# Two heads of a pair in the other order, and global scores as one block-diagonal product

## The chip, the cores and the metric

The kernel runs on one core of a Trainium2 chip. Its engines are TensorE (the matrix unit, PE in the profile; its weight loads are shown as PEld), VectorE (DVE), ScalarE (ACT), GpSimd (POOL) and SyncE (SP, which issues the transfers here). TensorE multiplies a stationary operand of up to 128 rows by 128 columns with a moving operand and adds into PSUM, from where DVE and ACT read. The metric is the device time in microseconds of one execution.

## The reference

Four sequences (B = 4) with 8 heads of 64 each hold 512 local and 32 global tokens. Global queries attend to all 544 keys; local ones attend to the 32 global keys and to a window of 32 keys on either side. The result, 2304 tokens of 512 features, goes through two feed-forward stages:

```python
s_g = scale * np.matmul(q_g, k_all.transpose(0, 1, 3, 2))     # global scores
out_g = np.matmul(sm(s_g), v_all)
s_ll = np.where(mask, scale * np.matmul(q_l, k_l.transpose(0, 1, 3, 2)), -1e9)
a_l = sm(np.concatenate([s_lg, s_ll], axis=-1))               # s_lg: local queries on global keys
out_l = np.matmul(a_l, np.concatenate([v_g, v_l], axis=2))
...
h = np.maximum(x @ w_in, 0.0);  y = h * h @ w_out             # 512 -> 2048 -> 512
a, b = y @ w1, y @ w2                                         # 512 -> 1024
out = (a * b @ w3) @ w_out2                                   # -> 512
```

## The kernel before, in words

**Stages.** The kernel starts with attention of the first sequence and converts the first MLP's weights. Then a main list, the MLP's units for the blocks of one sequence (`h_unit`, first matrix, and `x_unit_a`, second matrix), is merged with a list of steps of attention for the next sequence (`cycle`, `merge`). So attention of sequences 1 to 3 runs beside the MLP of sequences 0 to 2, and all attention is over after some 330 us. Then follow the rest of the first MLP, the product of the last two matrices (`w_unit`), and the second MLP (`p_unit`, `x_add`).

**Pairs of heads.** The heads of a sequence are treated two at a time: pair j holds the heads 2j and 2j+1, called head 0 and head 1 in what follows. Queries and keys of a pair lie in one tile, head 0 in the rows 0 to 63, head 1 in the rows 64 to 127 (`ROWS`), with 64 features each. A product of one head's queries and keys thus uses 64 of TensorE's 128 rows, and two heads' products can run side by side. The first sequence (pairs 0 to 3) works on float32 as it was loaded (`kq_f`); one float32 product is two instructions in the trace. From pair 4 on, `emit_k` splits the raw tile (`kqraw`, two buffers) into a high and a low part (`kq_hl`, type float32r) on DVE, and a product is the sum of three passes, high by high, high by low, low by high (`PASSES`), of one instruction each. `emit_k` of pair n+1 is issued in the cycle of pair n, and then asks for the raw tile of the pair after.

**Steps of a pair.**
- `emit_g` (L213): scores of the 32 global queries of both heads against all keys, in two pieces of 288 and 256 keys. Before the change it reads the unsplit float32 tile for every pair. Four products, head by piece, are issued in turn so that the two heads work on different pieces; each takes 64 rows and 32 columns of the array, a quarter of its width. Softmax follows on DVE and ACT, into `pg`.
- `emit_s` (L200): scores of local queries, for 256 of them (a part), two groups of 128, into one PSUM tile for each head (`sc`); `soft` turns them into probabilities `p` (DVE, ACT, then a scaling on POOL at L195).
- `emit_t` (L261) transposes `p` of one head on TensorE (`tp`), and ACT copies it to `pt`; `emit_tg` does the same for `pg` (`tg`).
- `emit_pv` (L274): the products with the values, both heads into one PSUM tile `o`, head 0 in rows 0 to 63, head 1 in rows 64 to 127.
In a cycle the steps of pair n (global scores, local scores) and those of pair j = n-1 (transposes, value products) alternate; head 1's transposes of a part come after head 0's, just ahead of the value products of the second part.

**What sets the order.** The program order gives priorities, and a planner that simulates the engines' times places each instruction on its engine as soon as its operands and buffers are there in the simulation. So an instruction early in the program that must wait lets later ones pass. `in_turn` (L105) pins each product of a list behind the one before it, from the second product on; the first is free. On the chip each engine then takes its instructions in that order. The PSUM tiles `sc`, `sg`, `tg`, `tp` and `o` share one tag, `at`, with four buffers.

**POOL's work** in this stretch: the sums of converted weights (L395), the scaling (L195), squares (L434) and low parts (L103) for the MLP.

Of the kernel before, what the change touches and what calls it, by code (L numbers as in the profile page):

```python
# [9 lines left out]
F32 = mybir.dt.float32  # L10
F32R = mybir.dt.float32r
# [9 lines left out]
B, H, SL, SG, D = 4, 8, 512, 32, 64  # L21
S = SL + SG
# [29 lines left out]
HALF = 256  # L52
# [22 lines left out]
def attention_mlp(ctx: ExitStack, tc: tile.TileContext, kq0, kq, vw, wts, mask, ident, out):  # L75
    nc = tc.nc
# [9 lines left out]
    cv, rot, at = cv_cm.__enter__(), rot_cm.__enter__(), at_cm.__enter__()  # L86
# [4 lines left out]
    mask_sb = rot.tile([128, 4, 256], BF16, name="mask_sb")  # L91
    pg = rot.tile([128, 6, 128], F32, name="pg")


    sts = [rot.tile([128, 10], F32, name=f"st{k}") for k in range(ST_BUFS)]
    stgs = [rot.tile([64, 8], F32, name=f"stg{k}") for k in range(2)]
# [5 lines left out]
    def split_lo(eng, lo, raw, hi):  # L102
        eng.tensor_tensor(out=lo, in0=raw, in1=hi.bitcast(F32), op=ALU.subtract)  # L103

    def in_turn(products):  # L105

        for k, (o, w, x, start, stop) in enumerate(products):
            m = mm(o, w, x, start=start, stop=stop)  # L108
            if k:
                tc.keep_in_program_order(m)  # L110

    def chain(o, terms):
        for k, (w, x) in enumerate(terms):
            mm(o, w, x, start=(k == 0), stop=(k == len(terms) - 1))  # L114
# [4 lines left out]
    def xb(b):  # L119

        if b not in x_t:
            x_t[b] = sb.tile([128, 4, 2 * NB], F32, tag="xb", name="xb", bufs=2)
        return x_t[b]

    ROWS = [slice(64 * h, 64 * h + 64) for h in range(2)]
    kq_raw, kq_t, qg_t, v_t, p_t, pt_t = {}, {}, {}, {}, {}, {}

    def kq_tile(name, dtype=F32):
        return rot.tile([128, S + NK], dtype, tag="kq", name=name, bufs=KQ_BUFS)

    def load_pair(j, part):

        if part == 0:
            kq_raw[j] = kq_tile("kq_f32")
        t = kq_raw[j]
        c = slice(0, 608) if part == 0 else slice(608, HALF + NK + SG + HALF)
        nc.sync.dma_start(out=t[:, c], in_=kq0[j, :, c])  # L140
        q, k = t[:, :HALF] if part == 0 else t[:, HALF + NK :], t[:, HALF : HALF + NK]
        kq_t[j, part] = [(q, k)]
        qg_t[j] = q[:, :SG], k

    def load_kq(j):

        if H <= 2 * j < B * H:
            t = kq_raw[j] = pools["cv"].tile([128, S + NK], F32, tag="kqraw", name="kqraw", bufs=2)
            for h, r in enumerate(ROWS):
                src = kq[2 * j + h - H, r]  # L150
                nc.sync.dma_start(out=t[r, :HALF], in_=src[:, :HALF])
                nc.sync.dma_start(out=t[r, HALF:S], in_=src[:, HALF + NK :])
                nc.sync.dma_start(out=t[r, S:], in_=src[:, HALF : HALF + NK])
# [9 lines left out]
    def emit_k(j):  # L163

        raw = kq_raw.pop(j)
        hi, lo = (kq_tile("kq_hl", F32R) for _ in range(2))
        nc.vector.tensor_copy(hi, raw)
        split_lo(nc.vector, lo, raw, hi)
        for part, c in enumerate((slice(0, HALF), slice(HALF, S))):
            both = [(t[:, c], t[:, S:]) for t in (hi, lo)]  # L170
            kq_t[j, part] = [(both[a][0], both[e][1]) for a, e in PASSES]
        qg_t[j] = raw[:, HALF : HALF + SG], raw[:, S:]
        load_kq(j + 1)

    def soft(i, part, sc):
# [24 lines left out]
    def emit_s(j, part):  # L200

        terms = kq_t[j, part]
        sc = [ps.tile([128, 2, 256], F32, tag="at", name="sc", bufs=AT_BUFS) for _ in ROWS]
        at_q, at_k = (128 * n + SG * part for n in range(2)), KSTART[2 * part : 2 * part + 2]
        in_turn(
            (o[:, n, :], x[r, c : c + 128], y[r, w : w + 256], k == 0, k == len(terms) - 1)
            for n, (c, w) in enumerate(zip(at_q, at_k))
            for k, (x, y) in enumerate(terms) for o, r in zip(sc, ROWS)
        )
        for h, o in enumerate(sc):  # L210
            soft(2 * j + h, part, o)

    def emit_g(j):  # L213

        q, keys = qg_t.pop(j)
        sg = [ps.tile([128, 512], F32, tag="at", name="sg", bufs=AT_BUFS) for _ in range(2)]

        pf = pg.rearrange("p c k -> p (c k)")
        tail = pf[:, 288:736].rearrange("p (a c) -> p a c", a=2)[:, :, :128]
        pieces = (  # L220
            (sg[0][:, :288], lambda x: x[:, :288], pf[:, :288]),
            (
                sg[1][:, :256].rearrange("p (a c) -> p a c", a=2),
                lambda x: x[:, 256:576].rearrange("p (a c) -> p a c", a=2)[:, :, 32:160],
                tail,
            ),
        )
        products = []
        for turn in range(2):
            for h, r in enumerate(ROWS):  # L230
                s, of_keys, _ = pieces[(turn + h) % 2]
                products.append((s[SG * h : SG * (h + 1)], q[r], of_keys(keys[r]), True, True))
        in_turn(products)
        st = stgs[j % 2]
        for k in range(2):
            nc.vector.tensor_reduce(
                out=st[:, k : k + 1], in_=sg[k][:64, : 256 + 32 * (1 - k)], axis=AX.X, op=ALU.max
            )
        nc.vector.tensor_reduce(out=st[:, 2:3], in_=st[:, 0:2], axis=AX.X, op=ALU.max)
        nc.vector.tensor_scalar_mul(st[:, 2:3], st[:, 2:3], -SCALE)  # L240
        for k, (s, _, p) in enumerate(pieces):
            nc.scalar.activation(
                p[:64], s[:64], AF.Exp, bias=st[:, 2:3], scale=SCALE, accum_out=st[:, 3 + k : 4 + k]
            )
        nc.vector.tensor_reduce(out=st[:, 6:7], in_=st[:, 3:6], axis=AX.X, op=ALU.add)
        nc.vector.reciprocal(st[:, 6:7], st[:, 6:7])
        nc.vector.tensor_scalar_mul(pf[:64, :640], pf[:64, :640], st[:, 6:7])
# [26 lines left out]
    def emit_pv(j, part, alone=False):  # L274

        b, heads = 2 * j // H, (2 * j, 2 * j + 1)
        o = ps.tile([128, 2, 160], F32, tag="at", name="o", bufs=AT_BUFS)


        both, local, glob = slice(0, 160), slice(0, 128), slice(128, 160)  # L280
        if part == 0:
            m = local if alone else both
            groups = ((0, 0, m), (0, 1, m)), ((1, 6, local), (1, 7, local))
        else:
            more = (0, 1, 4) if alone else (4,)
            groups = (
                ((0, 2, both), *((0, c, glob) for c in more), (0, 3, both)),
                ((1, 5, local), (1, 4, local)),
            )
        in_turn(  # L290
            (o[r, n, m], v_t[i][:, VPOS[c], :], pt_t[i][:, c, m], k == 0, k == len(g) - 1)
            for g in groups for k, (n, c, m) in enumerate(g) for i, r in zip(heads, ROWS)
        )
        s = part * (HALF + SG)
        x = xb(b)[:, j % (H // 2)]
        nc.scalar.copy(x[:, s : s + HALF].rearrange("p (n q) -> p n q", n=2), o[:, :, :128])
        g = x[:, HALF : HALF + SG]
        if part == (1 if alone else 0):
            nc.vector.tensor_copy(g, o[:, 0, 128:])
        elif part == 1:  # L300
            nc.vector.tensor_tensor(out=g, in0=g, in1=o[:, 0, 128:], op=ALU.add)
        if part == 1 or alone:
            for i in heads:
                del pt_t[i], v_t[i]
# [17 lines left out]
    def cycle(j, ahead=True, behind=True):  # L322
# [31 lines left out]
        if ahead and not native and n + 1 < B * H // 2:  # L354
            steps.insert(3, lambda: emit_k(n + 1))
# [143 lines left out]


    load_pair(0, 0)
    nc.sync.dma_start(out=mask_sb, in_=mask)
    nc.sync.dma_start(out=ident_sb, in_=ident)
    load_pair(1, 0)
    load_w(0)
    load_v(0, 0)
    load_v(1, 0)
    load_w(1)
    load_pair(2, 0)
    load_pair(3, 0)  # L510
    load_v(2, 0)
# [3 lines left out]
    for t in stgs:  # L515
        nc.gpsimd.memset(t, 1e-9)
    nc.vector.memset(pg, 0.0)

    def xcols(i):
        s, n = block(i)  # L520
        s -= S * (i // 2)
        return x_t[i // 2][:, :, s : s + n]
# [18 lines left out]
    def end_a(i, d, o):  # L541
        (nc.scalar.copy if d < 2 or i < SHARED else nc.vector.tensor_copy)(staged(i, d), o)
        if d == 3:
            nc.sync.dma_start(out=of(part_d, i), in_=st_t[0])

    def split_a(i, d):
        if i < NBLK:
            split_x(i, d, xcols(i)[:, d])
        else:
            split_x(i, d, x_t[0][:, 0, d])  # L550
# [12 lines left out]
    for i in range(0, NBLK, 2):  # L563
        main = []
        for j in (i, i + 1):
            if j >= SHARED:
                main += rows(
                    j, 0, 8, lambda d, j=j: split_a(j + 1, d), lambda d, j=j: end_a(j, d, acc[d])
# [204 lines left out]
```

## Time and profile before

| | |
|---|---|
| median of three runs | 925.94 us (922.17 to 926.93) |
| the profiled execution | 921.11 us, span 919.0 us |
| TensorE, its weight loads | busy 891.2 us (97%), 789.2 us (86%) |
| DVE, ACT, POOL | 398.2 us (43%), 478.2 us (52%), 284.8 us (31%) |
| mean granted TensorE clock | 0.994 |

The span runs from the first to the last instruction of the profiled execution. In the timeline a row gives start and length in us, engine, line, operation, what is written and read, the part of the array (128*64: 128 rows and 64 columns), the moving operand, and how many instructions were merged into the row. The end of a TensorE row is modelled and lies a little behind the start of the next.

### The profile page before, as it was taken

Reading aid. Unit: us, or ns where it says so; the run is one execution under the profiler, and the core shown is the slowest. Engines: PE = TensorE matmul, PEld = TensorE weight load, DVE = VectorE, ACT = ScalarE, POOL = GpSimd, SP = SyncE. Lnnn points to the kernel's source line nnn. Section 1 sums busy time; section 2 is a strip of 40 time slices with the busy share of each in tenths; the row PEclk is TensorE's granted clock in tenths of the full one; section 3 lists DMA queues with packets and bytes.
Section 4 is the critical chain, followed back from the end, with each engine's and each line's share of the span. In section 5 each row is a group of like instructions: output and inputs, shape, how many; then the busy total and the mean of one; then the engine's idle time right before and its main releaser. Section 6 shows DMA issues by size and latency. Waiting matters only on the chain.

```text
span 919.0 us, 15988 instructions
## 1 busy us (share of the span) xinstructions
PE 891.2 (97%) x6128; PEld 789.2 (86%) x6128; DVE 398.2 (43%) x1019; ACT 478.2 (52%) x1235; POOL 284.8 (31%) x280
## 2 busy tenths in 40 slices
PE   6799999999999999999999999999999999999998
PEld 3577787888888899999988899999988888888886
DVE  6996554563164336676544456564010200201201
ACT  6887666756375657886655558764111211212111
POOL 4594541635163522322222222210111111111111
PEclk9899999999999999999999999999999999999999
DMA  7643313232124227335544445545000200100101
GB/s 253 217 133 92 97 49 123 74 98 95 50 52 132 79 73 237 130 133 180 191 144 166 162 136 182 180 158 169 1 24 1 87 1 0 44 1 1 44 1 43
DMA packets 52347, 92.58 MB, mean 101 GB/s; under 512 B 4400, under 2 KB 35248, under 8 KB 52272
## 3 DMA queue, kind: packets, MB, share of 16 engines
q1 hardware_dynamic: 52272, 91.57, 30.3%
q8 instruction: 48, 0.79, 0.3%
q14 instruction: 27, 0.22, 0.1%
HBM read 71.63 MB, written 19.92 MB: 100 GB/s over the span
## 4 chain that ended last, share of the span: by engine, by line
PE 68%; ACT 10%; DMA 10%; DVE 5%; POOL 3%; issue 2%; SPq 1%; ACTq 0%; POOLq 0%; DVEq 0%
PE ab L114 21%; PE acc L465 15%; PE h L114 12%; DMA wraw<-in_wts 9%; PE x L114 7%; PE o L108 4%; PE sc L108 3%; PE tp L267 3%; ACT wt L372 2%; PE sg L108 2%; POOL wt L395 2%; ACT wt L375 2%; DVE wt L385 2%; ACT r L431 1%; ACT hl L432 1%
## 5 line engine op out<-in xcount | busy, mean ns | idle before, releaser
L395 POOL TENSOR_TENSOR wt<-wt 128x512 int32<-128x512 int32 x72 | 100.0, 1389 | 232.1 <-DVE wt L385 172.2
L114 PE MATMUL h<-hl,ua 128*128 128x256 f32 (+1 forms) x768 | 122.6, 300 | 3.0 <-DVE hl L103 2.0
L677 DVE TENSOR_TENSOR r<-r,ab 128x480 f32<-128x480 f32 (+1 forms) x40 | 24.3, 607 | 219.7 <-PE ab L114 219.0
L114 PEld LDWEIGHTS h<-hl,ua 128*128 128x128 f32 x768 | 103.7, 191 | 15.0 <-issue 6.4
L114 PE MATMUL h<-hl,va 128*128 128x256 f32 (+1 forms) x768 | 111.3, 289 | 2.4 <-ACT r L431 2.4
L465 PE MATMUL acc<-hl,vb 128*128 128x256 f32 (+1 forms) x768 | 110.5, 289 | 1.7 <-DVE hl L103 1.7
L114 PEld LDWEIGHTS h<-hl,va 128*128 128x128 f32 x768 | 102.5, 188 | 4.6 <-ACT r L431 3.5
L465 PEld LDWEIGHTS acc<-hl,vb 128*128 128x128 f32 x768 | 102.2, 189 | 4.1 <-DVE hl L103 2.5
L103 POOL TENSOR_TENSOR hl_c<-r,hl_c 128x480 fp32r<-128x480 f32 x32 | 39.2, 1225 | 210.8 <-ACT hl_c L679 203.0
L465 PE MATMUL acc<-hl_c,wv 128*128 128x480 f32 x384 | 89.2, 380 | 0.0
L114 PE MATMUL x<-hl,ub 128*128 128x288 f32 (+1 forms) x576 | 86.9, 296 | 2.0 <-POOL hl L103 2.0
L114 PE MATMUL ab<-hl_c,ua 128*128 128x480 f32 x384 | 87.1, 380 | 0.0
L195 POOL TENSOR_TENSOR p<-p,st 128x512 f32<-128x512 f32 x56 | 62.4, 1125 | 79.4 <-ACT p L185 27.3
L114 PE MATMUL ab<-hl_c,ub 128*128 128x480 f32 x384 | 86.6, 380 | 0.0
L114 PEld LDWEIGHTS x<-hl,ub 128*128 128x128 f32 x576 | 76.0, 189 | 7.7 <-POOL hl L103 2.6
L114 PEld LDWEIGHTS ab<-hl_c,ub 128*128 128x128 f32 x384 | 72.0, 188 | 11.9
L114 PEld LDWEIGHTS ab<-hl_c,ua 128*128 128x128 f32 x384 | 71.9, 188 | 11.9
L465 PEld LDWEIGHTS acc<-hl_c,wv 128*128 128x128 f32 x384 | 72.0, 188 | 11.4
L676 ACT COPY r<-ab 128x480 f32<-128x480 f32 (+1 forms) x40 | 20.9, 523 | 116.3 <-PE ab L114 113.7
L372 ACT ACTIVATE wt<-wraw 128x512 f32<-128x512 f32 x72 | 48.6, 676 | 55.3 <-DMA wraw<-in_wts 50.9
L185 ACT ACTIVATE p<-p,st 128x256 f32<-128x256 f32 x128 | 64.0, 503 | 24.8 <-DVE st L181 24.8
L103 POOL TENSOR_TENSOR hl<-r,hl 128x256 fp32r<-128x256 f32 (+1 forms) x56 | 48.2, 866 | 47.2 <-ACT hl L679 45.8
(90 smaller groups left out, 1362.0 us busy)
## 6 DMA issues: line engine op xcount, KB each, us to landing
wraw<-in_wts SPq DMA_DIRECT2D x72, 512.0 KB, 3.4
v_f<-in_vw SPq DMA_DIRECT2D x24, 256.0 KB, 2.9
x2l<-x_d SPq DMA_DIRECT2D x4, 960.0 KB, 5.8
out<-y SPq DMA_DIRECT2D x16, 240.0 KB, 2.3
kqraw<-in_kq SPq DMA_DIRECT2D x24, 144.0 KB, 2.9
x_d<-xb SPq DMA_DIRECT2D x4, 576.0 KB, 4.6
part_d<-st SPq DMA_DIRECT2D x4, 576.0 KB, 3.6
xl<-x_d SPq DMA_DIRECT2D x4, 576.0 KB, 5.2
```

The source lines that it names most:

```text
L103: eng.tensor_tensor(out=lo, in0=raw, in1=hi.bitcast(F32), op=ALU.subtract)
L108: m = mm(o, w, x, start=start, stop=stop)
L114: mm(o, w, x, start=(k == 0), stop=(k == len(terms) - 1))
L185: nc.scalar.activation(p[:, n, :], p[:, n, :], AF.Exp, bias=least[:, n : n + 1], scale=-1.0, accum_out=sums[:, n, 0:1],)
L195: nc.gpsimd.tensor_tensor(out=p, in0=p, in1=over.unsqueeze(2).to_broadcast([128, 2, 256]), op=ALU.mult)
L267: nc.tensor.transpose(tp[:, k, :], p[:, t % 2, 128 * half : 128 * (half + 1)], ident_sb)
L372: first = nc.scalar.activation(t[0].bitcast(F32), raw[:, :, 1].bitcast(F32), AF.Copy, scale=2.0**-112)
L375: nc.scalar.activation(t[2], raw[:, :, 0].bitcast(U32), AF.Copy, scale=2.0**-29)
L395: nc.gpsimd.tensor_tensor(out=b, in0=b, in1=m, op=ALU.add)
L465: mm(acc[d], w[:, a, 128 * d : 128 * (d + 1)], g_t[f][:, b], start=(f + k == 0), stop=(f + k == 9),)
L676: nc.scalar.copy(r, a)
L677: nc.vector.tensor_tensor(out=r, in0=r, in1=b, op=ALU.mult)
```

## The change

`HEADS = (1, 0)`: in `emit_s` and `emit_pv`, head 1's product of each step is issued before head 0's. In `emit_g` POOL copies the 32 global queries of both heads into a 128x128 tile that is otherwise zero, head 0 in rows 0 to 63 and columns 0 to 31, head 1 in rows 64 to 127 and columns 32 to 63. One product with all 128 rows of keys then gives both heads' scores in rows 0 to 63 of the result. For pairs 0 to 3 the tile is float32 (`qgf`), two copies and two products a pair; from pair 4 on it is float32r (`qgp`, a high and a low plane), four copies, and three passes on either piece, six products. The split tile takes the place of the raw one, which `emit_g` no longer reads. The tiles have one buffer each and are set to zero once, on POOL.

```diff
+    qgp = rot.tile([128, 2, 128], F32R, name="qgp")
+    qgf = [at.tile([128, 128], F32, name="qgf")]
...
+    HEADS = (1, 0)
...
-        qg_t[j] = q[:, :SG], k
...
-        qg_t[j] = raw[:, HALF : HALF + SG], raw[:, S:]
...
-            for k, (x, y) in enumerate(terms) for o, r in zip(sc, ROWS)
+            for k, (x, y) in enumerate(terms) for o, r in ((sc[h], ROWS[h]) for h in HEADS)
...
-        q, keys = qg_t.pop(j)
+        terms = kq_t[j, 1]
+        qs = qgf if len(terms) == 1 else [qgp[:, 0], qgp[:, 0], qgp[:, 1]]
+        for q, (x, _) in list(zip(qs, terms))[:: 2]:
+            for h, r in enumerate(ROWS):
+                nc.gpsimd.tensor_copy(q[r, SG * h : SG * (h + 1)], x[r, :SG])
...
-        products = []
-        for turn in range(2):
-            for h, r in enumerate(ROWS):
-                s, of_keys, _ = pieces[(turn + h) % 2]
-                products.append((s[SG * h : SG * (h + 1)], q[r], of_keys(keys[r]), True, True))
-        in_turn(products)
+        for k, (s, of_keys, _) in enumerate(pieces):
+            chain(s, [(q, of_keys(y)) for q, (_, y) in zip(qs, terms)])
...
-            for g in groups for k, (n, c, m) in enumerate(g) for i, r in zip(heads, ROWS)
+            for g in groups for k, (n, c, m) in enumerate(g)
+            for i, r in ((heads[h], ROWS[h]) for h in HEADS)
...
+    nc.gpsimd.memset(qgf[0], 0.0)
+    nc.gpsimd.memset(qgp.bitcast(F32), 0.0)
```

## Rows read from the trace of the kernel before

**Rows 1.** Busy time of the engines by stretch, with granted clock and DMA share
```profile
36.00:84.00 48.00, 43.83 (x336) 34.46 (x334) 41.49 (x106) 40.07 (x115) 35.06 (x30) 0.96 0.47 148
84.00:330.00 246.00, 243.99 (x2071) 204.79 (x2071) 113.29 (x445) 150.00 (x478) 110.16 (x127) 1.00 0.26 82
```
**Rows 2.** The chain of waits by line, of 36 to 84, then of 110 to 330
```profile
by line: POOL wt L395 15.6%; POOL r L434 8.0%; POOL hl L103 7.7%; PE o L108 6.5%; PE x L114 6.5%; PE h L114 6.4%; PE sc L108 5.7%; PE sg L108 5.6%; POOL p L195 5.2%; ACT p L185 4.1%; ACT pg L242 4.1%; PE tp L267 4.1%; ACT wt L372 3.8%; issu
...
by line: PE h L114 26.8%; PE x L114 26.4%; PE o L108 14.8%; PE sc L108 10.8%; PE tp L267 10.3%; PE sg L108 6.3%; PE tg L255 2.1%; DVE kq_hl L103 0.6%; POOL p L195 0.5%; DVE p L181 0.3%; issue 0.3%; DVE kq_hl L167 0.3%; DVE hl L103 0.2%; DVE
```
**Rows 3.** TensorE in order of time, 92 to 96 and 99 to 102
```profile
93.23 1.11 PE L108 MATMUL sg<-kqraw 64*32 64x288 f32 x8
94.26 1.54 PE L108 MATMUL o<-pt_f,v_f 128*64 128x160 f32 x26
...
99.88 1.79 PE L108 MATMUL sg<-kqraw 64*32 64x288 f32 x8 [0.17 <-DMA v_f<-in_vw]
```
**Rows 4.** TensorE in order of time, global scores in two pieces
```profile
119.42 0.67 PE L108 MATMUL sg<-kqraw 64*32 64x288 f32 x2
120.02 0.66 PE L114 MATMUL h<-hl,ua 128*128 128x288 f32 x3
...
122.24 1.10 PE L108 MATMUL sg<-kqraw 64*32 64x256 f32 x6
```
**Rows 5.** TensorE in order of time, local scores: undisturbed, the first split, the start of the last
```profile
108.88 0.98 PE L108 MATMUL sc<-kq_hl 64*128 64x256 f32 x12
...
127.12 0.38 PE L108 MATMUL sc<-kq_hl 64*128 64x256 f32 x1
127.43 1.05 PE L114 MATMUL x<-hl,ub 128*128 128x288 f32 x6
128.41 0.97 PE L108 MATMUL sc<-kq_hl 64*128 64x256 f32 x11
...
303.51 0.38 PE L108 MATMUL sc<-kq_hl 64*128 64x256 f32 x1
```
**Rows 6.** TensorE in order of time, value products: undisturbed, a split, the start of the last
```profile
112.68 1.20 PE L108 MATMUL o<-pt_f,v_f 128*64 128x160 f32 x16
...
116.83 0.49 PE L108 MATMUL o<-pt_f,v_f 128*64 128x160 f32 x2
...
121.00 1.31 PE L108 MATMUL o<-pt_f,v_f 128*64 128x160 f32 x18
...
322.63 0.49 PE L108 MATMUL o<-pt_f,v_f 128*64 128x160 f32 x2
```
**Rows 7.** The chain of waits, stretches of twelve MLP products: 256 columns, then 288
```profile
393.13 1.41 PE acc L465 x12
...
573.35 1.59 PE acc L465 x12
```
**Rows 8.** Groups of weight loads, 84 to 330: busy us, mean ns, idle before
```profile
L114 PEld LDWEIGHTS h<-hl,ua 128*128 128x128 f32 x468 | 62.8, 188 | 8.2 <-issue 4.7 <-ACT pt_f L259 0.5 <-ACT r L431 0.5
...
L108 PEld LDWEIGHTS sg<-kqraw 64*32 64x32 f32 x96 | 5.5, 105 | 5.7 <-DVE st L181 0.9 <-PE o L108 0.7 <-issue 0.5
```
**Rows 9.** Groups of instructions on POOL, whole span
```profile
L395 POOL TENSOR_TENSOR wt<-wt 128x512 int32<-128x512 int32 x72 | 100.0, 1389 | 232.1 <-DVE wt L385 172.2 <-ACT wt L375 26.7 <-ACT hl L432 11.2
L195 POOL TENSOR_TENSOR p<-p,st 128x512 f32<-128x512 f32 x56 | 62.4, 1125 | 79.4 <-ACT p L185 27.3 <-DVE st L189 19.5 <-PE o L108 17.0
L434 POOL TENSOR_TENSOR r<-r 128x256 f32<-128x256 f32 x24 | 17.2, 724 | 23.2 <-ACT hl L432 23.2
L516 POOL MEMSET stg<- 64x8 f32 x2 | 0.1, 98 | 0.0
```
**Rows 10.** Raw keys and their split in order of time, 81 to 103: DVE, SP, then the chain
```profile
83.79 1.32 DVE L103 TENSOR_TENSOR kq_hl<-kqraw,kq_hl 128x1120 fp32r<-128x1120 f32 x1
...
94.40 0.49 SPq L151 DMA_DIRECT2D kqraw<-in_kq  x1
...
99.31 2.87 DMA kqraw<-in_kq
```

More of the change, by code (lines that the diff above doesn't have):

```diff
@@ L128, in attention_mlp @@
     ROWS = [slice(64 * h, 64 * h + 64) for h in range(2)]
-    kq_raw, kq_t, qg_t, v_t, p_t, pt_t = {}, {}, {}, {}, {}, {}
+    HEADS = (1, 0)
+    kq_raw, kq_t, v_t, p_t, pt_t = {}, {}, {}, {}, {}
     def kq_tile(name, dtype=F32):
```

## The prediction

> **What bounds the kernel now.** I read first the busy time by stretch [rows 1], then what the chain of waits is made of inside the stretches [rows 2], then TensorE in order of time where attention runs beside the first MLP [rows 3 to 6]. The edits reach only the first 330 us: attention is over there, and the 589 us behind it keep their instructions. In 84:330 TensorE is busy 243.99 of 246.00 us at granted clock 1.00 and every other engine at most 61% (ACT 150.00 of 246) [rows 1]; from 110 on, the chain is TensorE's own work for over 95% [rows 2]. So there a TensorE microsecond saved should be a microsecond saved. In 36:84 the chain is led by POOL (15.6% + 8.0% + 7.7% + 5.2%) and TensorE holds about a third [rows 2]; 0:36 is start-up. There TensorE time is mostly cover, and new POOL work may cost.
>
> The timeline shows something that busy shares hide: TensorE is busy, but not at full use. A pair of heads is meant to run as two half-array products side by side. Often the first product of head 0 stands alone, microseconds ahead of the rest [rows 4 to 6], with MLP products between. The planner let it go as soon as its own operands were there; head 1's came later, and only the products after the first are pinned to their predecessor. The lone product uses half the array, and each trip into the half-array form and back costs extra.
>
> **The yardstick.** A 128x128 product in a stream costs 1.41/12 = 0.118 us with 256 columns and 1.59/12 = 0.132 us with 288 [rows 7].
>
> **Part 1, global scores on the whole array.** Per pair eight instructions of 64*32 go (four float32 products, two instructions each). Undisturbed they hold TensorE from 93.23 to 94.26, 1.03 us, where the row says 1.11: such a row ends 0.07 or so behind the next start [rows 3]. Of the 12 pairs in 84:330, five run so; six are split: 0.60 (119.42 to 120.02) + 1.03 (the row of 1.10) = 1.63 us; one, at 99.88, has its stall inside, 1.72 [rows 3, 4]. Sum 5 x 1.03 + 6 x 1.63 + 1.72 = 16.6 us. They are 18 trips into another array form; for a lone score product in part 2 entry and return come to some 0.2 us together (0.50 less the 0.31 from 127.12 to 127.43 [rows 5]); I take 0.15, 2.7 us. Before: 19.3 us.
> After, for these 12 pairs: three passes on two pieces, 3 x 0.132 + 3 x 0.118 = 0.75 us, 9.0 us in all, and about 0.1 us of changeover where a neighbour is a half-array product, 1.2 us. Saved: 9 us. Bounds: at worst a whole-array group costs what an undisturbed group costs now, 1.03 us, and still can't be hurt by a split (saved 5.7); at best it pays no changeover (10.3).
> Weight loads grow from 32 to 128 columns, 105 to 188 ns each [rows 8]. In the stream of rows 7 loads of 188 ns follow every 118 ns and hide, so I charge none; unhidden, six would make 1.13 us a pair and take 12 x 0.38 = 4.6 us off the sum. The Trainium skill, "TensorE: Matmul & The Clock Gate", section "LDWEIGHTS (loading the stationary operand)", says that a load's time follows the columns and not the rows, by its formula an estimated 27 against 107 ns. That speaks against the change; the trace agrees in direction and has 105 against 188.
>
> **The copies in front of it.** Each pair now starts with POOL copies of 64x32: two for the four pairs of 0:84, four for the others, 56 in all, and two memsets at the start, while the first loads are under way. No row has this copy: below stands POOL's small memset, 98 ns, above its 128x256 product, 724 ns [rows 9]. I take 0.15, near the memset, since 32 columns are few: 48 x 0.15 = 7.2 us in 84:330, where POOL is busy 110.16 of 246 us (at 724 ns, 35 us, it still fits). Behind them queue the softmax scaling (L195) and the MLP's low parts (L103), before the product waits. TensorE's new wait is for hi and lo from DVE, then POOL. The DVE split of a pair is made well ahead (that of the pair scored at 93.23 ends at 85.11 [rows 3, 10]), so only POOL's queue is left; between 110 and 330 TensorE hardly ever waits for POOL (0.5% of the chain [rows 2]). In 36:84 it costs: 8 copies, 1.2 us (0.8 to 5.8), set against gains there.
> One thing comes free: raw keys were held until the global scores had read them. The load at 94.40 starts as the scores that began at 93.23 end; the last piece of that tile takes 2.87 us on the chain at 99.31, to 102.18 [rows 10], and the pair's split waits for it. Read by the split alone, the buffer would be free at 85.11, 9 us earlier. I credit 1 us (0 to 3).
>
> **Part 2, head 1 first in the local scores.** Undisturbed, twelve products take 0.98 less 0.07, 0.91 us [rows 5]. Split: the lone one starts at 127.12, six x products follow, the other eleven start at 128.41: 1.29 - 6 x 0.132 = 0.50 us for the lone product with both changeovers, and the eleven still take 0.97 less 0.07, 0.90, for 0.01 less. There are 16 such splits in 84:330, the last at 303.51 [rows 5]: 16 x 0.49 = 7.8 us. What head 1 lacks here is not data (both heads come with one tile) but its PSUM buffer, one of four under a tag that all of attention shares. If buffers go round in the order in which tiles are made, head 1's is the later, head 1 first waits for both, and the splits vanish. If whichever asks first gets the first free one, head 1 takes it and head 0 is late: saved nothing. On TensorE the tiles of this tag are first written in program order throughout, which fits both. I take the first.
>
> **Part 3, head 1 first in the value products.** Here head 1 truly is late: its transposes are issued last, and ACT has to copy them out. Split: two instructions (one float32 product) at 116.83, 0.49 less 0.07 = 0.42 us, and eighteen at 121.00 [rows 6]; with the 0.2 of changeovers from the scores the two cost 0.62. Being gone from the rest, they give back something: sixteen take 1.13 us, eighteen staggered 1.24, and twenty in step, none of which the trace has, by my estimate 1.13 plus two more pairs at the 0.11 that the two extra instructions add between those rows, 1.35. So a split costs 0.62 - 0.11 = 0.5 us, at least 0.3 (0.42 less 0.11), and 16 of them stand in 84:330, the last at 322.63 [rows 6]: 7.2 us at 0.45 (4.8 to 9.6). Head 1's operands are simulated times of the planner; if ACT is late on the chip, TensorE waits as it did at the second product.
>
> **Sum.** 9 + 7.8 + 7.2 + 1 = 25 us in 84:330; in 0:84 splits go too (three float32 score splits, two of values), but POOL leads, so I put nothing there (-3 to +5). Removed work must be followed by work that is ready: the MLP blocks need finished attention, and a shorter TensorE lays bare some of the softmax latency. I let 85% through, 21 us. The profiled execution took 921.1 us (span 919.0), so 900; the median of the three runs is 925.9, 4.8 above it, so 905. I say **904 us**, and 896 to 911 for this case alone.
>
> **Rivals.**
> *A: buffers go to whoever asks first.* Local score splits stay; 9 + 7.2 + 1 = 17, through 85% 14.6: 911 us. For it: both heads' operands are one tile. Against: no score tile is written ahead of an earlier made one.
> *B: attention's latency becomes the bound.* TensorE idles at the end of each sequence; if half goes through, 12.5 us: 913. For: at 99.31 the chain does hold a transfer [rows 10]. Against: rows 1, ACT at 61%.
> *C, the other side: the copies stall TensorE.* TensorE is in order; a copy queued behind a weight sum (1.39) and a scaling (1.13) [rows 9] with its three followers at 0.15 is 3.1 us late if the planner misjudged POOL. In 16 pairs that is 50 us against 25: 950. It decides at 25/16 = 1.6 us of stall a pair; at 2.2 us it is 935. For: 36:84, where POOL leads. Against: POOL waits rather than is waited for from 110 on.
> *D: packing was worth its factor.* If the quarter-array products had run four abreast, the whole array with zeros would double their time: 12 x 1.03 lost rather than 9 gained, 25 - 9 - 12 = 4 us: 922, no change. Against: eight instructions take 1.03 us while two alone hold 0.60 [rows 3, 4], so two ran abreast, no more. The Trainium skill, "TensorEngine Tiling (Array Packing)", section "Theoretical Speedup", promises up to twofold for one dimension of at most 64 and fourfold for one of at most 32; by it this change gives speed away, and the trace shows about the twofold alone.
>
> **Chances.** Forecast 0.60, A 0.18, B 0.11, C 0.07, D 0.04. One measurement of this kernel can't tell less than 0.5%, 4.6 us, from no change. Faster: the first three nearly whole, 0.86. Same: D, the weak end of B, C below its deciding point, 0.08. Slower: C, 0.06. Range 893 to 919: it takes in A and B, and at its low end all 25 us with the early loads' 3 and the best ends of parts 1 and 3.
>
> **What would show it.** Global scores: six whole-array instructions a pair over about 0.75 us, apart or together, with TensorE waiting on POOL copies nowhere over 1 us. No lone local score and no pair of lone value instructions in 84:330 (the lone score, now of head 1, would show A). Attention ends some 20 us earlier, with the stretch behind it at 589 us as now. TensorE idle over 5 us between 110 and the end of attention would show B; waits for the copies over 1.6 us a pair, C; a later stretch that grows by as much as the first shrinks would make the prediction wrong in a way that I have no rival for.

## The result and the profile after

The changed kernel takes 910.08 us (910.03 to 911.75), the kernel before beside it 924.06 (920.29 to 926.93): ratio 0.986 [0.981, 0.990], some 14 us faster where 21 were forecast. The time lies in the range and near rival A's 911. The two profiled executions are 921.11 us (span 919.0) and 910.03 us (span 908.2); the rows below are of these.

The first view is the head of the page: span, busy time and share of each engine.

```profile
span 908.2 us, 15938 instructions
PE 872.0 (96%) x6088; PEld 788.2 (87%) x6088; DVE 394.2 (43%) x1019; ACT 480.0 (53%) x1235; POOL 297.9 (33%) x338
```

TensorE's busy time fell from 891.2 to 872.0 us, 19.2 us, but the span by only 10.8: TensorE's idle time (span less busy) grew by 8.4, from 27.8 to 36.2 us. (By the medians the time fell by 14.0; the profiled execution of the kernel before lies 3 us below its median, so up to 3 of the 8.4 may belong to that execution.) Where it grew is read from TensorE's busy time by stretch: window, its length, busy us (instructions), granted clock, DMA share, GB/s. First the kernel before:

```profile
0.00:36.00 36.00, 22.80 (x120) 0.91 0.68 227
36.00:110.00 74.00, 68.35 (x558) 0.98 0.43 135
110.00:330.00 220.00, 219.47 (x1849) 1.00 0.25 79
```

The same stretches of the changed kernel:

```profile
0.00:36.00 36.00, 19.50 (x98) 0.95 0.65 219
36.00:110.00 74.00, 65.51 (x543) 0.98 0.46 141
110.00:330.00 220.00, 217.66 (x1950) 1.00 0.26 81
```

Window less busy gives the idle time: 13.20, 5.65 and 0.53 us before, 16.50, 8.49 and 2.34 after. Of the 8.4 us more, 6.1 come before 110 us, where POOL and loads lead, and 1.8 between 110 and 330. In 110:330 a hundred instructions more fit into the same time: that stretch gained and the start lost.

Next is TensorE in order of time, one pair, answering to [rows 3 to 6]: start, length, line, operation, out<-in, part of the array.

```profile
116.60 1.20 PE L111 MATMUL o<-pt_f,v_f 128*64 128x160 f32 x16
117.73 0.40 PE L117 MATMUL h<-hl,ua 128*128 128x288 f32 x1
118.06 0.38 PE L111 MATMUL sc<-kq_hl 64*128 64x256 f32 x1
118.37 0.80 PE L117 MATMUL h<-hl,ua 128*128 128x288 f32 x4
119.10 0.97 PE L111 MATMUL sc<-kq_hl 64*128 64x256 f32 x11
...
123.92 1.32 PE L111 MATMUL o<-pt_f,v_f 128*64 128x160 f32 x20
125.17 0.52 PE L258 MATMUL tg<-ident_sb,pg 64*128 64x64 f32 x5
125.62 1.03 PE L117 MATMUL sg<-kq_hl,qgp 128*128 128x288 f32 x6
126.48 0.70 PE L117 MATMUL x<-hl,ub 128*128 128x288 f32 x4
```

- The value products stand together: twenty in step hold TensorE from 123.92 to 125.17, 1.25 us. None of the 16 lone pairs of instructions of before is left.
- The global scores are six whole-array instructions, from 125.62 to 126.48, 0.86 us, against 1.03 undisturbed and 1.63 split before.
- The local scores are still split: one product at 118.06, four MLP products, eleven at 119.10. There were 16 lone ones in 84:330 before and there are 16 now; as the kernel issues head 1 first and only the first product of a turn is free, they are head 1's.

Last, what TensorE waited for between 110 and the end of attention: total, times, longest.

```profile
PE tp L270 <- POOL p L198: 1.3, 1, 1.3
PE h L117 <- ACT hl L425: 1.1, 2, 0.7
```

There is no wait for a copy in it.

### The profile page after: what moved, and what is told of

It reads as the page before. It is cut to its first block, busy times and chain, and to the rows that moved or that the text cites. A ratio compares the mean times of both kernels' runs of the same rounds, so it can differ in the third digit from the quotient of the medians.

```text
span 908.2 us, 15938 instructions
## 1 busy us (share of the span) xinstructions
PE 872.0 (96%) x6088; PEld 788.2 (87%) x6088; DVE 394.2 (43%) x1019; ACT 480.0 (53%) x1235; POOL 297.9 (33%) x338
## 4 chain that ended last, share of the span: by engine, by line
PE 70%; DMA 12%; ACT 8%; DVE 4%; POOL 3%; issue 2%; SPq 1%; ACTq 0%; POOLq 0%; DVEq 0%
PE ab L117 21%; PE acc L469 16%; PE h L117 13%; DMA wraw<-in_wts 10%; PE x L117 8%; PE o L111 4%; PE sc L111 3%; PE tp L270 3%; ACT wt L376 2%; ACT wt L379 2%; DMA w_d<-ws 1%; PE sg L117 1%; DVE wt L389 1%; ACT r L435 1%; ACT hl L436 1%
## 5 line engine op out<-in xcount | busy, mean ns | idle before, releaser
L399 POOL TENSOR_TENSOR wt<-wt 128x512 int32<-128x512 int32 x72 | 96.6, 1342 | 234.5 <-DVE wt L389 177.1
L117 PE MATMUL h<-hl,ua 128*128 128x256 f32 (+1 forms) x768 | 118.7, 296 | 7.1 <-ACT hl L425 4.1
L184 DVE CUSTOM_DVE_ANT_0 p<-sc,mask_sb 128x256 f32<-128x256 f32 x128 | 46.6, 420 | 45.8 <-PE sc L111 44.7
```

The lines of the kernel that those rows point to most:

```text
L184: nc.vector.tensor_tensor_reduce(out=p[:, n, :], in0=sc[:, n, :], in1=mask_sb[:, 2 * part + n, :], scale=-SCALE, scalar=3.0e38, op0=ALU.ad ...
L399: nc.gpsimd.tensor_tensor(out=b, in0=b, in1=m, op=ALU.add)
```

## The experiments

The medians of the kernel before beside them were 923.5 to 923.8 us. Diffs are against the changed kernel unless another is named.

**Value products alone**, against the kernel before:

```diff
+    HEADS = (1, 0)
...
-            for g in groups for k, (n, c, m) in enumerate(g) for i, r in zip(heads, ROWS)
+            for g in groups for k, (n, c, m) in enumerate(g)
+            for i, r in ((heads[h], ROWS[h]) for h in HEADS)
```

> The kernel before with head 1 first in the value products alone. Theory (the value products' splits and the global scores pay, the local scores' order does nothing, the start loses some 5 us to the early copies of queries): no lone value product is left, 16 splits at about 0.6 us, and fewer split global scores, so 9 to 11 us faster, 915 to 917; the first global scores start near 36 us as before. Rival (the local scores' order carries a good part): 5 us or less here.

Measured: 911.16 us, ratio 0.987 [0.984, 0.989]. TensorE's busy time is 881.3 us, 9.9 less than before. The gain of 12.6 us is more than I expected. The global scores of pair 5, at 99.9 us before, start at 104.9 here, so this order makes them late without any copy.

**Global scores alone** (both products back to head 0 first):

```diff
-            for k, (x, y) in enumerate(terms) for o, r in ((sc[h], ROWS[h]) for h in HEADS)
+            for k, (x, y) in enumerate(terms) for o, r in zip(sc, ROWS)
...
-            for g in groups for k, (n, c, m) in enumerate(g)
-            for i, r in ((heads[h], ROWS[h]) for h in HEADS)
+            for g in groups for k, (n, c, m) in enumerate(g) for i, r in zip(heads, ROWS)
```

> The changed kernel with head 0 first again in both places: only the global scores on the whole array, with their copies. Theory: 6 to 7 us of TensorE less between 84 and 330, 4 to 5 us lost before 84 because POOL's copies stand early in its queue: 2 to 3 us faster, within what can't be told from no change. Rival (the start of the changed kernel is late for another reason than the copies): 6 us or more faster, and the first global scores start near 36 us.

Measured: 913.82 us, ratio 0.989 [0.987, 0.991]; busy 881.4, 9.8 less than before. I expected 2 to 3 us; the gain of 9.9 is the rival's. The two parts add up in TensorE's work (9.9 + 9.8 = 19.7 against 19.2 for the whole change) and not in time: 12.6 and 9.9 us alone by the medians, some 14 together. Something in the whole change eats work that each part alone saves. With this kernel the global scores of pair 5 start at 97.6 us, with the whole change at 106.7, and before at 99.9: the late start comes from the order of the heads and not from the copies.

**Local scores back to head 0 first**, the rest as changed:

```diff
-            for k, (x, y) in enumerate(terms) for o, r in ((sc[h], ROWS[h]) for h in HEADS)
+            for k, (x, y) in enumerate(terms) for o, r in zip(sc, ROWS)
```

> The changed kernel with head 0 first again in the local scores alone. Theory (whichever head asks first takes the free buffer, so a lone product stands ahead in either order): the same number of lone scores, now of head 0, and the time of the changed kernel within 3 us, ratio 0.983 to 0.989. Rival (buffers go round in order, the flip did something): 4 us or more slower than the changed kernel.

Measured: 908.96 us, ratio 0.983 [0.981, 0.986], the same time as the changed kernel. TensorE in order of time:

```profile
117.96 0.38 PE L111 MATMUL sc<-kq_hl 64*128 64x256 f32 x1
118.27 0.94 PE L117 MATMUL h<-hl,ua 128*128 128x288 f32 x5
119.14 0.97 PE L111 MATMUL sc<-kq_hl 64*128 64x256 f32 x11
```

The same split, now of head 0; 18 such lone products stand in 84:330. The edit also takes back the order of the first sequence's local scores, so the equal time was tested in the stretches. Of the stretch 0:84 this is the line of the changed kernel, then that of this one (busy us and instructions of PE, PEld, DVE, ACT and POOL, granted clock, DMA share, GB/s):

```profile
0.00:84.00 84.00, 59.21 (x412) 46.10 (x412) 64.93 (x164) 63.69 (x169) 58.17 (x67) 0.96 0.55 180
0.00:84.00 84.00, 61.98 (x406) 49.67 (x407) 61.58 (x164) 63.71 (x169) 57.72 (x67) 0.86 0.51 170
```

Ahead of 84 us TensorE did about the same work, here at a lower granted clock and so with more busy and less idle time; behind 84 us it is busy 813.3 us here and 812.8 with the change. So what is late is not a certain head but whichever is issued second, as rival A has it: the first to ask takes the PSUM buffer that comes free first.

**A claiming product.** If that is so, a short product ahead of the turn that asks for head 0's buffer, with the real ones pinned behind it, takes the early buffer, stands alone itself, and leaves the twelve together. Its 8 columns are overwritten by the scores; from pair 4 on:

```diff
+        claim = [(sc[0][:, 0, :8], qgp[:, 0], qgp[:, 1, :8], True, True)] if len(terms) > 1 else []
...
-            (o[:, n, :], x[r, c : c + 128], y[r, w : w + 256], k == 0, k == len(terms) - 1)
+            claim
+            + list((o[:, n, :], x[r, c : c + 128], y[r, w : w + 256], k == 0, k == len(terms) - 1)
...
```

> The changed kernel, and ahead of the local scores of the pairs from 4 on one whole-array product of 8 columns that takes head 0's buffer (its value is overwritten), so that head 1's first product waits for both buffers. Theory: the 16 lone scores at 0.50 us go, 24 short products at 0.1 to 0.15 us come: 4 to 5 us faster than the changed kernel, ratio near 0.980. Rival (a lone score costs nothing, since its time would else be a wait): 0 to 3 us slower than the changed kernel.

Measured: 900.75 us, ratio 0.976 [0.973, 0.978], 9.3 below the changed kernel by the medians. TensorE in order of time:

```profile
116.94 0.17 PE L111 MATMUL sc<-qgp 128*128 128x8 f32 x1
116.96 0.38 PE L117 MATMUL h<-hl,ua 128*128 128x288 f32 x1
117.27 0.97 PE L111 MATMUL sc<-kq_hl 64*128 64x256 f32 x12
```

The claiming product is let go one MLP product ahead of the twelve here, the next row starts 0.02 us behind it, and no lone local score is left. The gain is twice the 4 to 5 us that I expected. Over the whole span busy time is 867.0 us, 5.0 less than with the changed kernel, and idle time 31.9, 4.3 less; but these totals mix two clocks, as the stretch 0:84 shows:

```profile
0.00:84.00 84.00, 61.96 (x414) 48.67 (x415) 65.34 (x164) 63.88 (x170) 58.92 (x67) 0.88 0.54 178
```

Up to 84 us two instructions more than with the changed kernel took 2.75 us more, at a granted clock of 0.88 against 0.96. Behind 84 us, where the clock was 1.00 up to 330, TensorE is busy 7.7 us less (805.1 against 812.8) and idle 1.6 us less. So the 16 splits cost about what the prediction priced them at, 7.8 us, and the claiming products less than the 0.1 to 0.15 us each that I had set against it.

**The first sequence's values in the old order.** The late start of pair 5 has two suspects: the values' order in the first sequence, and the POOL copies of pair 0, which run at 14.99 us for a product at 41.1. The first suspect is undone here:

```diff
-            for i, r in ((heads[h], ROWS[h]) for h in HEADS)
+            for i, r in ((heads[h], ROWS[h]) for h in ((0, 1) if alone else HEADS))
```

> The changed kernel with head 0 first again in the value products of the first sequence (pairs 0 to 3); from pair 4 on as changed. Theory (the late start comes from the values' order in the first sequence: the loads of values wait longer for products that end later, and weight loads stand behind them): the global scores of pair 5 start at 97 to 101 us instead of 106.7, the time falls by 4 to 6 us, ratio 0.979 to 0.982. Rival (POOL's early copies make the start late): pair 5's global scores still start after 104 us, time within 2 us of the changed kernel.

Measured: 905.85 us (903.79 to 908.09), ratio 0.981 [0.978, 0.983], 4.2 below the changed kernel by the medians; pair 5 is at 101.4. TensorE by stretch:

```profile
0.00:36.00 36.00, 19.23 (x97) 0.96 0.65 219
36.00:110.00 74.00, 68.86 (x558) 0.95 0.48 146
110.00:330.00 220.00, 218.69 (x1945) 1.00 0.26 80
```

Idle time of 36:110 is 5.14 us, as before the change (5.65), against 8.49; some of that may be the lower clock (0.95 against 0.98), but the instructions done are 558, as before the change, against 543. In this stretch TensorE's transposes wait 0.4 us for POOL's scaling, 3.0 in the changed kernel. Idle time of 0:36 stays at 16.77. So this order costs in 36:110, and the loss in 0:36 has another cause.

**Copies pinned**, on top of the claiming product, so that they can't run ahead of older POOL work:

```diff
-                nc.gpsimd.tensor_copy(q[r, SG * h : SG * (h + 1)], x[r, :SG])
+                tc.keep_in_program_order(nc.gpsimd.tensor_copy(q[r, SG * h : SG * (h + 1)], x[r, :SG]))
```

> The kernel with the short claiming product, and POOL's copies of queries pinned behind what stands ahead of them in the program, so that those of pair 0 no longer run at 15 us ahead of a weight sum. Theory (values' order): the start stays late, time within 2 us of 900.8. Rival (early copies): pair 5's global scores start 4 us or more earlier, 895 to 898.

Measured: 899.87 us, ratio 0.975 [0.973, 0.978]. The copies of pair 0 moved, from 14.11 us with the claiming product alone to 37.59, and the global scores of pair 5 stay at 106.0 (105.9): the time does not change, and the second suspect falls.

**Claiming product with the first sequence's values in the old order, and with the pinned copies besides.** Edits as above, together.

> Short claiming product and the first sequence's values in the old order, from pair 4 on head 1 first. If both gains add up, 4 to 6 us below 900.8: 895 to 897, ratio near 0.970. If the early copies make the start late: 899 to 902.

> Short claiming product, old values' order in the first sequence, and pinned copies. Theory (values' order alone makes the start late): as the kernel without pinning, 895 to 897. Rival (copies): 895 to 897 too, but then pinning alone gives the same and the old order alone does not.

Measured: 899.40 us, ratio 0.974 [0.972, 0.976], and 899.20, ratio 0.974 [0.972, 0.976]. Both miss the 895 to 897. By the first of these texts 899.4 speaks for the early copies, but pinning them gains nothing here either (0.2 us). Pair 5 does start earlier, at 100.8 and 101.3, and the old order gives only 1.4 us, not the 4.2 that it gave without the claiming product: the two savings overlap, and why was not taken apart.

**Changed order from pair 4 on alone**: the first sequence's local scores in the old order too, on top of the first of these two:

```diff
-            for k, (x, y) in enumerate(terms) for o, r in ((sc[h], ROWS[h]) for h in HEADS)
+            for k, (x, y) in enumerate(terms) for o, r in ((sc[h], ROWS[h]) for h in (HEADS if claim else (0, 1))))
```

> Short claiming product; heads in the changed order only from pair 4 on, local scores and values of the first sequence in the old order. Theory (the flip of the local scores delays the first transposes by 1 to 2 us, since six kernels with it have them at 13.2 to 14.4 us and three without at 12.1 to 12.8; the values' order costs the rest of the late start): first transposes near 12.3 us, TensorE's idle time before 36 us near 14 us, 1 to 3 us below the 899.4 of the kernel with the old values' order alone: 896 to 898. Rival (the first transposes vary from run to run): no change from 899.4.

Measured: 895.61 us (895.13 to 895.93), ratio 0.970 [0.968, 0.971], the fastest of all, 14.5 us below the changed kernel. The loss in 0:36 is seen where the first transposes start. First the changed kernel, DVE, POOL and TensorE in order of time; the brackets hold the wait before an instruction and what ended it.

```profile
9.12 0.43 DVE L384 TENSOR_SCALAR wt<-wt 128x512 int32<-128x512 int32 x1 [1.75 <-ACT wt L376]
10.66 0.16 DVE L192 TENSOR_REDUCE st<-st 128x2 f32<-128x4 f32 x1 [1.12 <-ACT p L188]
10.75 0.69 DVE L389 SCALAR_TENSOR_TENSOR wt<-wraw,wt 128x512 int32<-128x512 int32 x1
...
11.59 1.28 POOL L399 TENSOR_TENSOR wt<-wt 128x512 int32<-128x512 int32 x1 [10.11 <-DVE st L193]
12.81 2.23 POOL L198 TENSOR_TENSOR p<-p,st 128x512 f32<-128x512 f32 x2
...
14.10 2.12 PE L270 MATMUL tp<-ident_sb,p 128*128 128x128 f32 x8 [5.09 <-POOL p L198]
```

The same places with the changed order from pair 4 on alone:

```profile
8.84 0.43 DVE L386 TENSOR_SCALAR wt<-wt 128x512 int32<-128x512 int32 x1 [1.57 <-ACT wt L378]
9.30 0.69 DVE L391 SCALAR_TENSOR_TENSOR wt<-wraw,wt 128x512 int32<-128x512 int32 x1
...
10.14 1.26 POOL L401 TENSOR_TENSOR wt<-wt 128x512 int32<-128x512 int32 x1 [8.67 <-DVE wt L391]
11.37 2.22 POOL L198 TENSOR_TENSOR p<-p,st 128x512 f32<-128x512 f32 x2
...
12.46 2.29 PE L272 MATMUL tp<-ident_sb,p 128*128 128x128 f32 x8 [3.48 <-POOL p L198]
```

In the changed kernel a softmax sum stands on DVE ahead of a weight step and waits 1.12 us for ACT; the weight step behind it starts at 10.75 instead of 9.30, POOL's weight sum at 11.59 instead of 10.14, and POOL's scaling and the transposes follow 1.4 to 1.6 us late. This divides all kernels of the study: in the seven with the first sequence's local scores flipped the sum stands first, waits 1.11 to 1.12 us, and the transposes start at 13.2 to 14.4 us; in the five without (the one before among them) the weight step is first, and they start at 12.1 to 12.8. TensorE by stretch, with the order changed from pair 4 on alone:

```profile
0.00:36.00 36.00, 21.93 (x116) 0.94 0.64 223
36.00:110.00 74.00, 68.47 (x579) 0.98 0.45 145
110.00:330.00 220.00, 218.32 (x2015) 1.00 0.27 88
```

Idle time is 14.07, 5.53 and 1.68 us: ahead of 110 us that is 19.6, against 18.9 before the change and 25.0 after it.

**Copies twice.** Each copy is made twice, to test whether POOL's new work costs anything:

```diff
-                nc.gpsimd.tensor_copy(q[r, SG * h : SG * (h + 1)], x[r, :SG])
+                for _ in range(2):
+                    nc.gpsimd.tensor_copy(q[r, SG * h : SG * (h + 1)], x[r, :SG])
```

> The changed kernel with every one of POOL's copies of queries made twice, some 17 us more on POOL by the 238 and 651 ns that they took. Theory (POOL has room and the scores are placed late enough): within 3 us of the changed kernel's 910.1; in the first 84 us, where POOL leads, up to 3 us. Rival (the copies stand on TensorE's path): 8 us or more slower than the changed kernel.

Measured: 910.15 us, ratio 0.987 [0.984, 0.989], the time of the changed kernel. Groups of POOL's instructions (busy us, mean ns, idle before), first of the changed kernel, then with the copies doubled:

```profile
L222 POOL CAST qgp<-kq_hl 64x32 fp32r<-64x32 f32 x48 | 11.4, 238 | 22.3 <-PE sg L117 16.8 <-DVE kq_hl L171 3.8
L222 POOL COPY qgf<-kq_f 64x32 f32<-64x32 f32 x8 | 5.2, 651 | 1.5 <-PE sg L117 1.3
```

```profile
L223 POOL CAST qgp<-kq_hl 64x32 fp32r<-64x32 f32 x96 | 22.3, 232 | 23.8 <-PE sg L117 17.1 <-DVE kq_hl L171 2.4
L223 POOL COPY qgf<-kq_f 64x32 f32<-64x32 f32 x16 | 9.1, 571 | 3.6 <-PE sg L117 3.0
```

15 us more on POOL (31.4 against 16.6) cost nothing that can be measured.

## Why it came out so, step by step

**The yardstick, and what bounds the kernel.** Both held where they were read, in 84:330: TensorE is busy 243.47 us of it, before 243.99 [rows 1], and attention ends 10 us earlier: its last value products start at 316.19 us, before at 326.15. What follows them kept its time, 590.8 us (591.6 before), as forecast; the 20 us by which attention was to end earlier are 10. That end is no measure of the time by itself: with the copies pinned the last value products start at 319.59 us, and that kernel takes 899.87.

**Part 1, right.** Twelve pairs of global scores were priced at 0.75 us and 0.1 of changeover, 10.2 us. By the distance to the next row they take 0.86 us each (125.62 to 126.48), 10.26 in all, against 16.7 before. That is 6.4 of the 9 us forecast; the rest of the 9 is the price put on changeovers, which no row shows by itself. With this part alone TensorE's busy time fell by 9.8 us, the first sequence included. The weight loads as grown:

```profile
L117 PEld LDWEIGHTS sg<-kq_hl,qgp 128*128 128x128 f32 x72 | 9.8, 188 | 0.7 <-issue 0.2
```

They take 188 ns, as charged, and hide: six of them laid bare would make 1.13 us, not 0.86. The rule of the Trainium skill that spoke against it ("TensorE: Matmul & The Clock Gate", section "LDWEIGHTS (loading the stationary operand)": the time goes by the columns) holds in direction and cost nothing here. Rival D falls too. By "TensorEngine Tiling (Array Packing)" of the Trainium skill, section "Theoretical Speedup", a dimension of at most 32 allows up to fourfold speed, and then the whole array would have lost. In this trace a pair takes 0.86 us against 1.03 undisturbed. But this is no test of four abreast: in `emit_g` of the kernel before, head 0 always uses rows 0 to 63 of the array and gives rows 0 to 31 of a result, head 1 rows 64 to 127 and rows 32 to 63 of a result. All products of a pair thus share two places of the array, so no more than two could be side by side, and what four places would give was not tried. How much of the gain is the whole array and how much the passes of float32r in place of float32 instructions wasn't tried.

**The copies.** 0.15 us was too little: 238 and 651 ns in the mean, inside the bounds of 98 and 724. It made no difference, and the doubling shows that there is room for as much again. Rival C fails at its first condition, since no wait of TensorE for a copy stands among its waits up to 330 us. The raw keys' loads do come earlier (89.57 us, 94.40 before [rows 10]), but the scores of pair 5 began later (106.7 against 99.9), so the credit of 1 us shows nowhere.

**Part 2, the step that failed.** "If buffers go round in the order in which tiles are made ... the splits vanish. ... I take the first." They go to whichever asks first: 16 lone products before, 16 after, of the other head, and with the flip undone 18 of head 0 and the same time. The 7.8 us were not to be had by an order of heads. They were there, though: the claiming product takes off 7.7 us of busy time behind 84 us, and 9.3 us of the whole. My argument for the first reading, that score tiles were always written in the order of making, fits both, as I wrote, and so should have carried no weight.

**Part 3, right.** All 16 splits are gone. Twenty in step take 1.25 us, not 1.35; TensorE's busy time falls by 9.9 us with this part alone, the first sequence's included, where 7.2 were forecast for 84:330. ACT was not late: no wait of a value product stands among the waits between 110 us and the end of attention.

**The sum.** Without part 2 it is 17 us, and TensorE's busy time fell by 19.2. 85% was to go through; of 19.2 us 10.8 did by the two profiled executions (56%), 14 by the medians (73%). The other 8.4 are idle time, and not where I looked for it: 1.8 us of it in 110:330 (rival B asked for over 5), 6.1 ahead of 110 us, where I had "put nothing". Two edits in the first sequence bring most of it, neither of which gained anything there that these runs show. Its local scores in the new order move a DVE sum ahead of a weight step (shown above). Its values in the new order cost in 36:110, since with the old order alone idle time there falls from 8.49 to 5.14 us; the wait that goes is mainly that of the transposes for POOL's scaling, from 3.0 to 0.4 us, and from 3.0 to 0.4 with the claiming product too. What makes the scaling late stays open. With the values alone changed, value loads that wait on SP's queue hold back a weight load, and later TensorE waits for ACT, as these rows of SP's queue and of TensorE of that kernel show; but the changed kernel has no such wait on SP.

```profile
30.69 6.14 SPq L162 DMA_DIRECT2D v_f<-in_vw  x3
36.95 0.36 SPq L368 DMA_DIRECT2D wraw<-in_wts  x1
...
47.81 5.49 PE L114 MATMUL h<-hl,ua 128*128 128x256 f32 x24 [4.62 <-ACT r L433]
```

So the number is nearly rival A's 911, and for A's reason as to part 2; but A let 85% of 17 us through, 14.6, and the run reached 14 from a larger saving and a larger loss. That the two come out so close is luck.

## What to carry to other kernels

Where a planner gives rotating buffers to whoever asks first, issuing the other operand first moves a split and doesn't remove it; a tiny product that asks for the early buffer, with the real ones pinned behind it, does. An edit meant for a stretch that TensorE bounds should be kept to that stretch: the same edit in the start-up, where DVE, POOL and loads lead, reordered them and gave back a third of the TensorE time saved (6.1 of 19.2 us); with the claiming product, leaving the first sequence as it was took off 5.1 us (900.75 to 895.61). Two parts can be judged by adding their busy time; whether time adds up is read from the idle time by stretch, with the granted clock and the instructions done beside it, since a lower clock shows the same work as more busy and less idle time (61.96 us for 414 instructions at 0.88, 59.21 for 412 at 0.96).

## What was not expected of the hardware

A product of 8 columns on the whole array, put between whole-array products, costs next to nothing: in 18 of the 19 such places the next row starts 0.02 to 0.03 us later, while a lone half-array product of 256 columns among them cost 0.50 us with its changeovers [rows 5]. POOL's copies of 64x32 vary widely, from 201 to 1692 ns, and the float32 ones cost 651 ns in the mean against 238 for those that round to float32r; how much of this is other load at the start wasn't tried.
